# x @ w1 of the second layer of a mixture of experts as Strassen's seven block products over pairs of 512-token tiles

## The chip, the cores and the metric

One core of one Trainium2 chip runs the whole program. The metric is the time of one execution, in microseconds.

## What is computed

A transform of 8 x 3072 tokens of 256 features, then two mixtures of experts over the 24576 tokens, each of 8 experts with w1 of 256 x 1024 and w2 of 1024 x 256. In the first a token goes to one expert; in the second, which the change rewrites, every token goes through all of them and the results are weighted by a matrix P that is balanced in eight iterations.

```python
def _moe2_ref(x, w_gate, w1, w2):
    logits = x @ w_gate
    P = np.exp(logits - logits.max())
    for _ in range(8):
        P /= P.sum(1, keepdims=True) + 1e-09
        P /= P.sum(0, keepdims=True) + 1e-09
        P *= N / E
    for e in range(E):
        h = np.maximum(x @ w1[e], 0.0)
        ye = h @ w2[e]
        out += P[:, e:e + 1] * ye
```

## The kernel before

Products are taken in float32 from two parts: a value is hi + lo, where hi is what TensorE takes in one pass (fp32r), and a product is hi·hi + hi·lo + lo·hi, three matmuls.

The program has three stages, one behind another: the transform with the routing, the first layer (`First`, 50 tiles of 512 tokens that belong to one expert each), and the second layer (`Second`, 48 tiles of 512 tokens by 8 experts). `Second.run` (L792) goes over blocks of `NB` = 3 tiles; for a block it goes over the experts, up in one block and down in the next. Weights of an expert are loaded in two transfers (L707, L709, tiles `r`) and split by POOL (`split`, L490 and L491) for the expert after. For each expert and tile, `hidden` (L508) makes the hidden features, transposed, in 8 chunks of 128: six matmuls of 512 columns into one PSUM bank `ph` (L514), then ACT takes the relu into `hh` (L519) and DVE the rest into `hl` (L520). Then, for each of the tile's four blocks of 128 tokens, 8 chunks by two matmuls: `hh` by w2's hi and lo side by side, 512 columns (L857), and `hl` by w2's hi, 256 columns (L858). DVE adds both halves of the result, weighted by P, to `acc` (L873, L874). Rows of the finished tile are scattered to the output by POOL (L879). A tile's rows are loaded by SP (L803), transposed by PE and split by ACT and DVE (`transposed`, L499 to L503).

P is made in `sinkhorn` (L736): a generator whose steps are mixed into the first two experts of the first block, where results are kept unweighted (L860 to L863). An iteration is eight sums over experts on DVE (L767, L769), a reciprocal, eight products with column sums (L776), and one matmul (L782) that adds the column sums over the partitions.

In the first layer a tile is `hidden` as above and then, for each block of tokens, 8 chunks by three matmuls of 264 columns (L650 to L652). SP's order is the program's there; the other engines' instructions are placed by the scheduler. In the second layer all engines are placed by the scheduler, which keeps no engine's order fixed.

## Time and profile before

| | us |
|---|---|
| median of three runs | 10253.83 |
| lowest, highest | 10252.15, 10259.26 |
| profiled execution (its span) | 10260.5 |

The profile's page starts with the busy time of each engine, then shows the span in 40 slices, the DMA queues, the chain of work that ended last, the costliest groups and the DMA issues. PE is TensorE's matmuls, PEld its loads of stationary operands, DVE VectorE, ACT ScalarE, POOL GpSimd, SP SyncE, and SPq the queue of its DMAs. Groups read `out<-in`, by the names in the program, with partitions x elements. Matmuls overlap: their lengths on the page are longer than the distance between their starts.

### The profile page before, as it was taken

Reading aid. Unit: us, or ns where it says so; the run is one execution under the profiler, and the core shown is the slowest. Engines: PE = TensorE matmul, PEld = TensorE weight load, DVE = VectorE, ACT = ScalarE, POOL = GpSimd, SP = SyncE. Lnnn points to the kernel's source line nnn. Section 1 sums busy time; section 2 is a strip of 40 time slices with the busy share of each in tenths; the row PEclk is TensorE's granted clock in tenths of the full one; section 3 lists DMA queues with packets and bytes.
Section 4 is the critical chain, followed back from the end, with each engine's and each line's share of the span. In section 5 each row is a group of like instructions: output and inputs, shape, how many; then the busy total and the mean of one; then the engine's idle time right before and its main releaser. Section 6 shows DMA issues by size and latency. Waiting matters only on the chain.

```text
span 10260.5 us, 132706 instructions
## 1 busy us (share of the span) xinstructions
PE 10200.5 (99%) x54157; PEld 8686.2 (85%) x54157; DVE 4507.1 (44%) x8480; ACT 2598.8 (25%) x4731; POOL 2714.7 (26%) x2608
## 2 busy tenths in 40 slices
PE   9999999999999999999999999999999999999999
PEld 9799997888888888888888888888888888888888
DVE  5544446444444444444444444444444444444444
ACT  5444442222222222222222222222222222222222
POOL 3655553212222122222122221222212222212221
PEclk9999999999999999999999999999999999999999
DMA  6434442010100010000010000100000101000000
GB/s 174 155 136 138 137 138 78 25 38 33 38 33 30 33 38 33 38 33 36 27 40 31 35 28 33 38 33 38 33 29 33 38 34 38 26 37 33 34 33 15
DMA packets 194250, 525.92 MB, mean 51 GB/s; under 512 B 71617, under 2 KB 128098, under 8 KB 147778
## 3 DMA queue, kind: packets, MB, share of 16 engines
q1 hardware_dynamic: 167440, 464.96, 12.8%
q0 software_dynamic: 25632, 52.25, 1.6%
q8 instruction: 427, 7.00, 0.3%
q14 instruction: 189, 1.55, 0.0%
q10 hardware_dynamic: 562, 0.18, 0.0%
HBM read 433.16 MB, written 84.13 MB: 50 GB/s over the span
## 4 chain that ended last, share of the span: by engine, by line
PE 82%; issue 1%; DVE 0%; POOL 0%; ACT 0%; DMA 0%; POOLq 0%; SPq 0%
PE ph L514 41%; PE py L857 27%; PE py L858 14%; PE pt L501 0%; DVE S L769 0%; DVE P L776 0%; POOL out L879 0%; DVE r L773 0%; POOL w1l L491 0%; DVE acc L862 0%; DMA rows<-x 0%; ACT P L763 0%; DVE hl L520 0%; DVE S L767 0%; POOL w2b L491 0%
## 5 line engine op out<-in xcount | busy, mean ns | idle before, releaser
L519 ACT ACTIVATE hh<-ph 128x512 fp32r<-128x512 f32 x3472 | 2077.0, 598 | 6975.1 <-PE ph L514 6962.5
L520 DVE SCALAR_TENSOR_TENSOR hl<-ph,hh 128x512 fp32r<-128x512 f32 x3472 | 2399.9, 691 | 2922.7 <-ACT hh L519 2916.7
L514 PE MATMUL ph<-xh,w1h 128*128 128x512 f32 x6944 | 2767.4, 399 | 3.0 <-DVE hl L520 2.4
L514 PE MATMUL ph<-xh,w1l 128*128 128x512 f32 x6944 | 2737.2, 394 | 0.0
L514 PE MATMUL ph<-xl,w1h 128*128 128x512 f32 x6944 | 2726.7, 393 | 0.0
L857 PE MATMUL py<-w2a,hh 128*128 128x512 f32 x6144 | 2204.4, 392 | 0.0
L857 PE MATMUL py<-w2b,hh 128*128 128x512 f32 x6144 | 2198.9, 392 | 0.0
L858 PE MATMUL py<-w2a,hl 128*128 128x256 f32 x6144 | 1718.3, 280 | 0.0
L858 PE MATMUL py<-w2b,hl 128*128 128x256 f32 x6144 | 1718.2, 280 | 0.0
L490 POOL CAST w2b<-r 128x512 fp32r<-128x512 f32 x224 | 131.3, 615 | 5771.2 <-PE ph L514 5771.2
L873 DVE SCALAR_TENSOR_TENSOR acc<-py,P,acc 128x256 f32<-128x256 f32 x1332 | 644.0, 483 | 2236.2 <-PE py L858 2236.2
L514 PEld LDWEIGHTS ph<-xh,w1l 128*128 128x128 f32 x6944 | 1304.9, 188 | 332.6
L514 PEld LDWEIGHTS ph<-xh,w1h 128*128 128x128 f32 x6944 | 1304.7, 188 | 303.3 <-DVE hl L520 3.8
L514 PEld LDWEIGHTS ph<-xl,w1h 128*128 128x128 f32 x6944 | 1306.4, 188 | 292.7 <-DVE xl L491 0.5
L857 PEld LDWEIGHTS py<-w2b,hh 128*128 128x128 f32 x6144 | 1153.7, 188 | 254.9
L857 PEld LDWEIGHTS py<-w2a,hh 128*128 128x128 f32 x6144 | 1153.4, 188 | 253.7
L858 PEld LDWEIGHTS py<-w2a,hl 128*128 128x128 f32 x6144 | 1155.4, 188 | 14.2
L858 PEld LDWEIGHTS py<-w2b,hl 128*128 128x128 f32 x6144 | 1153.7, 188 | 0.0
L491 POOL TENSOR_TENSOR w1l<-r,w1h 128x512 fp32r<-128x512 f32 (+1 forms) x550 | 810.3, 1500 | 30.9 <-ACT w1h L490 29.8
L874 DVE SCALAR_TENSOR_TENSOR acc<-py,P,acc 128x256 f32<-128x256 f32 x1512 | 731.6, 484 | 54.0
L650 PE MATMUL py<-w2h,hh 128*128 128x264 f32 x1600 | 458.6, 287 | 0.0
L652 PE MATMUL py<-w2h,hl 128*128 128x264 f32 x1600 | 453.6, 284 | 1.8 <-DVE hl L520 1.8
(179 smaller groups left out, 5756.6 us busy)
## 6 DMA issues: line engine op xcount, KB each, us to landing
r<-m2w SPq DMA_DIRECT2D x226, 1024.0 KB
r<-m1w SPq DMA_DIRECT2D x100, 1024.0 KB
x<-y SPq DMA_DIRECT2D x50, 512.0 KB
xs<-zt SPq DMA_DIRECT2D x64, 384.0 KB
rows<-x SPq DMA_DIRECT2D x48, 512.0 KB
xt<-x SPq DMA_DIRECT2D x31, 768.0 KB
xt<-m1w2t SPq DMA_DIRECT2D x8, 1024.0 KB
tab<-z SPq DMA_DIRECT2D x8, 440.0 KB
```

What stands on the lines that cost most here:

```text
L490: (eng_hi.copy if hasattr(eng_hi, "copy") else eng_hi.tensor_copy)(hi, x)
L491: eng_lo.tensor_tensor(lo, x, hi.bitcast(F32), op=ALU.subtract)
L514: nc.tensor.matmul(p, w[:, k * 1024 + c * 128:k * 1024 + (c + 1) * 128], x[:, k, :], start=(i == 0), stop=(i == 5))
L519: nc.scalar.activation(hh, p, AF.Relu)
L520: nc.vector.scalar_tensor_tensor(hl, p, 0.0, hh.bitcast(F32), op0=ALU.max, op1=ALU.subtract)
L650: nc.tensor.matmul(p, hh, w2h[:, s], start=(c == 0), stop=False)
L652: nc.tensor.matmul(p, hl, w2h[:, s], start=False, stop=(c == 7))
L857: nc.tensor.matmul(p, hh, w2, start=(c == 0), stop=False)
L858: nc.tensor.matmul(p[:, 1, :], hl, w2[:, 0, :], start=False, stop=(c == 7))
L873: nc.vector.scalar_tensor_tensor(dst, p[:, 0, :], pe(e), dst, op0=ALU.mult, op1=ALU.add)
L874: nc.vector.scalar_tensor_tensor(dst, p[:, 1, :], pe(e), dst, op0=ALU.mult, op1=ALU.add)
```

## The change

A group of work is now one pair of tiles (`PAIR` = 8 blocks of 128 tokens), one expert and a quarter of its hidden features (256); 24 x 8 x 4 = 768 groups. Over it, x @ w1 is a product of 2 x 2 blocks: two halves of the 256 input features, two halves of the 256 hidden features, two tiles of tokens. `layer1` makes it from seven products (three matmuls of 512 columns each, L904) instead of eight. Sums of blocks of w1 and of x replace the blocks; sums of products are built in three PSUM banks `a`, `c` and `d`: a bank grows by a second, third or fourth product, and ACT copies it out at two points on the way (`kept`); a second copy goes straight into a sum. DVE adds copies to other banks (`total`, L921, tiles `z`). Of the four blocks of hidden features three come from `z` in SBUF and one from its bank; their relu on ACT and the rest `hl` on DVE (L916) follow.

`layer2` is h @ w2 for a group: for each of 8 blocks of tokens 2 x 3 matmuls of 256 columns (L958) into a half bank of `py`; the banks gather all four groups of an expert, and DVE adds them to `acc` after the fourth (L986). The second half of a group is placed between the products of the next (`turn`). PE's order in the second layer is now the program's (`manual_schedule`).

The seven sums of weight blocks, their hi and lo parts and w2's parts form a piece of 2816 floats on each of 128 partitions for each expert and quarter (`PIECE`). The generator `weights`, mixed into the first layer (`mix`), makes all 32 on ACT and DVE, two at a time, and stores them in DRAM (`wq`). The second layer loads one for each group, again for each pair, into a ring of three tiles. The sums of x are made by `prepare`: four blocks of four transposes, four differences and seven splits, by ACT and DVE for the first and second pair and by POOL for all others. In the first pair the results of experts 0 to 4 are copied to `held` and weighted later (`add_held`); the balancing of P has more, shorter steps, spread over the first groups, and what is left of it is emitted at the start of expert 3 (`HELD - 2`).

```diff
+            late = late(pool("mq", 1))
...
                 next(sp, None)
                 xt = ahead()
+                mix(2)
                 y = yp.tile([128, 4, 264], F32, name="y", tag="y")
...
                     nc.scalar.activation(y[:, j, :], p, AF.Copy, scale=ix[:, j, 2:3].bitcast(F32))
                     next(sp, None)
+                    mix(1)
...
+            def mix(n):
+                for _ in range(n):
+                    next(late, None)
...
-                xt = tile_(i, xt, self.split_weights(i + 1, nc.gpsimd) if i + 1 < NS else late, ahead)
+                xt = tile_(i, xt, self.split_weights(i + 1, nc.gpsimd) if i + 1 < NS else iter(()), ahead)
+            for _ in late:
...
+    def weights(self, pool):
+        store = None
+        for e in range(E):
+            for h in range(2):
...
+                yield
+                yield
+                if store:
+                    store()
+                yield
+                s = pool.tile([128, 2, 4, 128], F32, name="qs", tag="qs")
+                o = pool.tile([128, 2, PIECE], F32R, name="qo", tag="qo")
...
+                tt(s[:, :, 0, :], blk(1, 0), blk(1, 1), op=ALU.add)
+                tt(s[:, :, 1, :], s[:, :, 0, :], blk(0, 0), op=ALU.subtract)
+                yield
+                tt(s[:, :, 2, :], blk(0, 0), blk(1, 0), op=ALU.subtract)
+                tt(s[:, :, 3, :], blk(0, 1), s[:, :, 1, :], op=ALU.subtract)
+                yield
...
+                for hi, lo, v in parts:
+                    nc.scalar.copy(hi, v)
+                    yield
+                    tt(lo, v, hi.bitcast(F32), op=ALU.subtract)
+                    yield
+
+                def store(e=e, h=h, o=o):
+                    nc.sync.dma_start(self.wq[e, 2 * h:2 * h + 2].rearrange("j p c -> p j c"), o.bitcast(F32))
+        store()
...
             for e in range(1, E):
                 nc.vector.scalar_tensor_tensor(S, P[:, e, :], c[:, e:e + 1], S, op0=ALU.mult, op1=ALU.add)
-                if e in (3, 5):
+                if e % 2:
                     yield
             nc.vector.tensor_scalar_add(S, S, 1e-9)
+            yield
             nc.vector.reciprocal(r, S)
             yield
...
                 nc.vector.scalar_tensor_tensor(P[:, e, :], P[:, e, :], c[:, e:e + 1], r, op0=ALU.mult, op1=ALU.mult,
                                                accum_out=cs[:, e:e + 1])
-                if e in (2, 5):
+                if e % 2:
                     yield
+            yield
             yield
             p = psum.tile([128, 512], F32, name="psk", tag="ph")
             nc.tensor.matmul(p[:, 0:E], ones, cs, start=True, stop=True)
...
+            ring, xa, one, rowp, xbp = pool("nw", 3), pool("nxa", 1), pool("n1", 1), pool("nr", 1), pool("nb", 6)
+            ap_, hp, vp, zp = pool("na", 1), pool("nh", 10), pool("nv", 6), pool("nz", 6)
+            ctx.enter_context(tc.manual_schedule(engines={mybir.EngineType.PE}))
+            npair = TPP // PAIR
+            groups = [(b, e, j) for b in range(npair) for e in range(E) for j in range(4)]
+            loads = iter(groups)
+            ready = []
+            def load_weights():
+                g = next(loads, None)
+                if g:
+                    w = ring.tile([128, PIECE], F32R, name="w", tag="w")
+                    nc.sync.dma_start(w.bitcast(F32), self.wq[g[1], g[2]])
+                    ready.append(w)
...
+            def prepare(r, into, fast):
...
+                eh, el = (nc.scalar, nc.vector) if fast else (nc.gpsimd, nc.gpsimd)
+                new = lambda: xbp.tile([128, T], F32, name="xb", tag="xb")
+                def block(k, h):
+                    p = ph.tile([128, T], F32, name="pt", tag="ph")
+                    for i in range(4):
+                        nc.tensor.transpose(p[:, i * 128:(i + 1) * 128], r[:, 4 * h + i, k * 128:(k + 1) * 128], self.cst)
...
+                def keep(m, x):
+                    split(eh, el, hi[:, m, :], lo[:, m, :], x)
...
+                keep(6, b22)
+            def layer1(w, x, h):
+                hi, lo = x
+                wm = lambda part, m: w[:, part * W1P + m * 128:part * W1P + (m + 1) * 128]
+                def product(p, m, first):
+                    for n, (a, v) in enumerate(((0, hi), (0, lo), (1, hi))):
+                        nc.tensor.matmul(p, wm(a, m), v[:, m, :], start=first and n == 0, stop=n == 2,
+                                         skip_group_check=True)
+                def kept(p):
+                    v = vp.tile([128, T], F32, name="v", tag="v")
+                    nc.scalar.copy(v, p)
+                    return v
+                def done(i, half, z):
+                    hh = hp.tile([128, T], F32R, name="hh", tag="hh")
+                    hl = hp.tile([128, T], F32R, name="hl", tag="hl")
+                    nc.scalar.activation(hh, z, AF.Relu)
+                    nc.vector.scalar_tensor_tensor(hl, z, 0.0, hh.bitcast(F32), op0=ALU.max, op1=ALU.subtract)
+                    h[i, half] = hh, hl
+                def total(p, v):
+                    z = zp.tile([128, T], F32, name="z", tag="z")
+                    nc.vector.tensor_tensor(z, p, v, op=ALU.add)
+                    return z
+                new = lambda: ph.tile([128, T], F32, name="ph", tag="ph")
+                a = new()
+                product(a, 0, True)
+                v1 = kept(a)
+                yield
+                c = new()
+                product(c, 1, True)
+                done(0, 0, total(c, v1))
+                yield
+                product(a, 4, False)
+                v2 = kept(a)
+                yield
+                d = new()
+                product(d, 3, True)
+                yield
+                product(a, 5, False)
+                done(1, 1, total(d, kept(a)))
+                yield
+                product(a, 2, False)
+                done(1, 0, a)
+                yield
+                product(d, 6, False)
+                done(0, 1, total(d, v2))
+            def layer2(g, w, h, y, finish):
+                for q in range(PAIR):
+                    s = slice(q % 4 * 128, q % 4 * 128 + 128)
+                    out = y[q // 2][:, q % 2, :]
+                    for i in range(2):
+                        hh, hl = h[i, q // 4]
+                        w2h = w[:, 2 * W1P + i * D:2 * W1P + (i + 1) * D]
+                        w2l = w[:, 2 * W1P + (2 + i) * D:2 * W1P + (3 + i) * D]
+                        for n, (a, v) in enumerate(((hh, w2h), (hh, w2l), (hl, w2h))):
+                            nc.tensor.matmul(out, a[:, s], v, start=g[2] == i == n == q % 2 == 0,
+                                             stop=g[2] == 3 and i == 1 and n == 2, skip_group_check=True)
+                    if g[2] == 3 and q % 2:
+                        finish(q // 2)
+                    yield
...
+            sk = self.sinkhorn(one, hpool, ph, ones)
+            next(sk)
+            for _ in prepare(r, xa, True):
+                pass
+            held = []
+            turn = (0, 2, 0, 1, 2, 1, 2)
...
+            for g in groups:
+                b, e, j = g
+                w, h = ready.pop(0), {}
...
+                if j == 0:
+                    y = [py.tile([128, 2, D], F32, name="py", tag="py") for _ in range(4)]
+                    if b == 0 and e < HELD:
+                        if e == HELD - 2:
+                            for _ in sk:
+                                pass
...
+                    fin = finisher(g, y, acc if b or e >= HELD else None)
+                if (e, j) == (5, 0) and b + 1 < npair:
+                    r = load_rows(b + 1)
+                for n, _ in enumerate(layer1(w, x, h)):
+                    for _ in range(turn[n]):
+                        next(l2, None)
+                    if b == 0:
+                        next(sk, None)
+                        if late and e > HELD and not next(late[0], 1) is None:
+                            late.pop(0)
+                for _ in l2:
                     pass
+                load_weights()
...
+                if b + 1 < npair and (e, j) == ((7, 0) if b == 0 else (6, 0)):
+                    xprep = prepare(r, xb if b % 2 == 0 else xa, b == 0)
+                if e >= 6:
+                    for _ in range(4 if b == 0 else 1):
+                        next(xprep, None)
+                if (e, j) == (E - 1, 3):
+                    for _ in xprep:
                         pass
+                    x = xs.pop(0) if xs else None
+                l2 = layer2(g, w, h, y, fin)
...
+                pass
```

PE's order in a steady group, where `ph_41392` is bank a, `ph_41427` bank d, `w` a piece of weights and `py_40966` two blocks of the group before. Before, a chunk of `hidden` and the start of the next:

```order
L514 MATMUL ph_44716<-xh_42099,w1h_43950 128x512 [waits DVE_49]
L514 MATMUL ph_44716<-xl_42100,w1h_43950 128x512
L514 MATMUL ph_44716<-xh_42099,w1l_43951 128x512
L514 MATMUL ph_44716<-xh_42099,w1h_43950 128x512
L514 MATMUL ph_44716<-xl_42100,w1h_43950 128x512
L514 MATMUL ph_44716<-xh_42099,w1l_43951 128x512
L514 MATMUL ph_44727<-xh_42099,w1h_43950 128x512 [waits DVE_49]
```

Now, from product 4 to product 5:

```order
L904 MATMUL ph_41392<-xh_38062,w_41182 128x512 [waits Activation_49]
L904 MATMUL ph_41392<-xl_38063,w_41182 128x512
L904 MATMUL ph_41392<-xh_38062,w_41182 128x512
L904 MATMUL ph_41427<-xh_38062,w_41182 128x512
L904 MATMUL ph_41427<-xl_38063,w_41182 128x512
L904 MATMUL ph_41427<-xh_38062,w_41182 128x512
L958 MATMUL py_40966<-w_41080,hh_41298 128x256 x2
L958 MATMUL py_40966<-w_41080,hl_41299 128x256
L958 MATMUL py_40966<-w_41080,hh_41355 128x256 x2
L958 MATMUL py_40966<-w_41080,hl_41356 128x256
L904 MATMUL ph_41392<-xh_38062,w_41182 128x512 [waits Activation_49]
```

Six matmuls into one bank and then the next bank became three matmuls into a bank, three into another, one block of tokens of the second half, and the first bank again with a wait for ACT.

DVE's order in the second layer, where `py` are finished rows and `z` the sums that L921 makes. Before, between two tiles:

```order
L871 TENSOR_SCALAR acc_29810<-py_30308,P_21115 128x256 [waits PE_49]
L874 SCALAR_TENSOR_TENSOR acc_29810<-py_30308,P_21115,acc_29810 128x256 [waits DVE_49]
L520 SCALAR_TENSOR_TENSOR hl_30345<-ph_30337,hh_30344 128x512 [waits Activation_49]
L520 SCALAR_TENSOR_TENSOR hl_30356<-ph_30348,hh_30355 128x512 [waits Activation_49]
L520 SCALAR_TENSOR_TENSOR hl_30367<-ph_30359,hh_30366 128x512 [waits Activation_49]
```

Now, in a group that is the first of its expert:

```order
L921 TENSOR_TENSOR z_41334<-ph_41319,v_41332 128x512 [waits Activation_49]
L916 SCALAR_TENSOR_TENSOR hl_41337<-z_41334,hh_41336 128x512 [waits Activation_49]
L916 SCALAR_TENSOR_TENSOR hl_41356<-ph_41286,hh_41355 128x512 [waits Activation_49]
L921 TENSOR_TENSOR z_41368<-ph_41319,v_41317 128x512 [waits PE_49]
L916 SCALAR_TENSOR_TENSOR hl_41371<-z_41368,hh_41370 128x512 [waits Activation_49]
L921 TENSOR_TENSOR z_41402<-ph_41398,v_41396 128x512 [waits PE_49,Activation_49]
L916 SCALAR_TENSOR_TENSOR hl_41405<-z_41402,hh_41404 128x512 [waits Activation_49]
L986 SCALAR_TENSOR_TENSOR acc_38844<-py_40965,P_21425,acc_38844 128x256 [waits PE_49]
```

Where the rests `hl` followed one another, each from its bank, sums `z` stand between them, three of four `hl` read a `z`, and the sums of `acc` come behind, one for a block of tokens instead of two.

DVE's order where the balancing of P runs (`psk` is the bank of column sums, `cc` its reciprocal, `S` the row sums). Before, a whole start of an iteration with other work between:

```order
L783 TENSOR_SCALAR cc_21120<-psk_21575 128x8 [waits PE_49]
L784 RECIPROCAL cc_21120<-cc_21120 128x8 [waits DVE_49]
L785 TENSOR_SCALAR cc_21120<-cc_21120 128x8 [waits DVE_49]
L767 TENSOR_SCALAR S_21117<-P_21115,cc_21120 128x192 [waits DVE_49]
L862 TENSOR_TENSOR acc_21150<-py_21580,acc_21150 128x256 [waits Activation_49]
L769 SCALAR_TENSOR_TENSOR S_21117<-P_21115,cc_21120,S_21117 128x192 [waits DVE_49] x3
L520 SCALAR_TENSOR_TENSOR hl_21611<-ph_21603,hh_21610 128x512 [waits Activation_49]
L769 SCALAR_TENSOR_TENSOR S_21117<-P_21115,cc_21120,S_21117 128x192 [waits DVE_49] x2
L520 SCALAR_TENSOR_TENSOR hl_21622<-ph_21614,hh_21621 128x512 [waits Activation_49]
L769 SCALAR_TENSOR_TENSOR S_21117<-P_21115,cc_21120,S_21117 128x192 [waits DVE_49] x2
```

Now, at expert 3 of the first pair:

```order
L813 TENSOR_SCALAR cc_21430<-psk_22812 128x8 [waits PE_49]
L814 RECIPROCAL cc_21430<-cc_21430 128x8 [waits DVE_49]
L815 TENSOR_SCALAR cc_21430<-cc_21430 128x8 [waits DVE_49]
L795 TENSOR_SCALAR S_21427<-P_21425,cc_21430 128x192 [waits DVE_49]
L797 SCALAR_TENSOR_TENSOR S_21427<-P_21425,cc_21430,S_21427 128x192 [waits DVE_49] x7
L800 TENSOR_SCALAR S_21427<-S_21427 128x192 [waits DVE_49]
L802 RECIPROCAL r_21428<-S_21427 128x192 [waits DVE_49]
L805 SCALAR_TENSOR_TENSOR P_21425,cs_21431<-P_21425,cc_21430,r_21428 128x192 [waits DVE_49]
L805 SCALAR_TENSOR_TENSOR P_21425,cs_21431<-P_21425,cc_21430,r_21428 128x192 x7
L813 TENSOR_SCALAR cc_21430<-psk_22835 128x8 [waits PE_49]
```

The sums `hl` and of `acc` that stood between the steps are gone from there; an iteration stands whole, and the next behind it.

PE's order at the same places. Before, with one matmul of column sums:

```order
L857 MATMUL py_21580<-w2b_19587,hh_21456 128x512
L782 MATMUL psk_21575<-cs_21121,ones_81 128x8 [waits DVE_49]
L858 MATMUL py_21580<-w2b_19587,hl_21457 128x256
L857 MATMUL py_21580<-w2b_19587,hh_21467 128x512
L858 MATMUL py_21580<-w2b_19587,hl_21468 128x256
L514 MATMUL ph_21603<-xh_21471,w1h_19584 128x512 [waits Activation_49]
```

Now:

```order
L958 MATMUL py_22355<-w_22350,hl_22645 128x256
L812 MATMUL psk_22812<-cs_21431,ones_73 128x8
L812 MATMUL psk_22835<-cs_21431,ones_73 128x8 [waits DVE_49]
L812 MATMUL psk_22858<-cs_21431,ones_73 128x8 [waits DVE_49]
L812 MATMUL psk_22881<-cs_21431,ones_73 128x8 [waits DVE_49]
L904 MATMUL ph_22895<-xh_21436,w_22584 128x512 [waits DMAHW3_49]
```

One matmul among those of the second half became four in a row, three of them waiting for DVE, ahead of the next group's first product.

## Rows read from the trace of the kernel before

**Rows 1.** Page: busy time, chain that ended last, a group, DMA issues

```profile
PE 10200.5 (99%) x54157; PEld 8686.2 (85%) x54157; DVE 4507.1 (44%) x8480; ACT 2598.8 (25%) x4731; POOL 2714.7 (26%) x2608
...
PE 82%; issue 1%; DVE 0%; POOL 0%; ACT 0%; DMA 0%; POOLq 0%; SPq 0%
...
L874 DVE SCALAR_TENSOR_TENSOR acc<-py,P,acc 128x256 f32<-128x256 f32 x1512 | 731.6, 484 | 54.0
...
r<-m2w SPq DMA_DIRECT2D x226, 1024.0 KB
```

**Rows 2.** Timeline of PE, second layer: start, length (us), engine, line, operation

```profile
5002.11 0.39 PE L857 MATMUL py<-w2a,hh 128*128 128x512 f32 x1
...
5013.20 0.39 PE L514 MATMUL ph<-xh,w1h 128*128 128x512 f32 x1
...
5024.39 0.39 PE L857 MATMUL py<-w2a,hh 128*128 128x512 f32 x1
```

**Rows 3.** Timeline of PE, first layer: 24 matmuls of 264 columns between

```profile
1000.48 0.28 PE L650 MATMUL py<-w2h,hh 128*128 128x264 f32 x1
...
1003.38 0.39 PE L514 MATMUL ph<-xh,w1h 128*128 128x512 f32 x1
```

**Rows 4.** Timeline of all engines, first layer; in brackets idle time before, releaser

```profile
1004.54 0.40 PE L514 MATMUL ph<-xh,w1l 128*128 128x512 f32 x1
...
1004.98 0.60 ACT L519 ACTIVATE hh<-ph 128x512 fp32r<-128x512 f32 x1 [0.91 <-PE ph L514]
...
1005.61 0.69 DVE L520 SCALAR_TENSOR_TENSOR hl<-ph,hh 128x512 fp32r<-128x512 f32 x1 [10.42 <-ACT hh L519]
```

**Rows 5.** One line's instructions: shortest/median/longest ns, first and last start, shapes

```profile
L769 DVE SCALAR_TENSOR_TENSOR S<-P,cc,S x56: 401/419/1341, 1655.4 to 1777.0; 128x192 f32<-128x192 f32 x56
...
L491 POOL TENSOR_TENSOR w1l<-r,w1h x550: 1279/1302/2435, 437.2 to 10116.6; 128x512 fp32r<-128x512 f32 x151, 128x1024 fp32r<-128x1024 f32 x33
L491 DVE TENSOR_TENSOR xl<-pt,xh x196: 672/678/692, 432.4 to 9707.0; 128x512 fp32r<-128x512 f32 x196
L491 DVE TENSOR_TENSOR w2l<-g,w2h x50: 217/2452/2453, 363.7 to 1575.0; 128x64 fp32r<-128x64 f32 x50
```

**Rows 6.** One tile's instructions: issues of the raw weights, 3000 to 3600

```profile
L707 SPq DMA_DIRECT2D r<-m2w x7: 327/328/328, 3063.6 to 3534.3; - x7
L709 SPq DMA_DIRECT2D r<-m2w x7: 382/384/425, 3064.1 to 3534.7; - x7
```

**Rows 7.** Stretches: PE, PEld, DVE, ACT, POOL busy; granted clock, DMA share, GB/s

```profile
3066.00:3067.00 1.00, 1.00 (x6) 0.81 (x5) 0.69 (x1) 0.22 (x1) 1.00 (x2) 1.00 0.97 410
3070.00:3071.00 1.00, 1.00 (x6) 0.79 (x5) 0.69 (x1) 0.20 (x2) 0.00 (x0) 1.00 0.18 74
```

**Rows 8.** Timeline of DVE, first layer, one tile behind the last of rows 4

```profile
1029.28 0.69 DVE L520 SCALAR_TENSOR_TENSOR hl<-ph,hh 128x512 fp32r<-128x512 f32 x1 [10.42 <-ACT hh L519]
```

**Rows 9.** Timeline where the second layer starts (1615 to 1645)

```profile
1622.58 0.28 PE L652 MATMUL py<-w2h,hl 128*128 128x264 f32 x1
...
1629.62 0.82 SPq L803 DMA_DIRECT2D rows<-x  x2
...
1633.31 1.94 PE L501 MATMUL pt<-ident,rows 128*128 128x128 f32 x8 [10.45 <-DMA rows<-x]
```

**Rows 10.** Waits of PE: waiting group, releaser: us in all, count, longest

```profile
PE psk L782 <- DVE P L776: 8.1, 2, 6.3
```

**Rows 11.** Timeline of DVE, balancing of P (1655 to 1690)

```profile
1674.68 0.15 DVE L783 TENSOR_SCALAR cc<-psk 128x8 f32<-128x8 f32 x1
...
1676.47 0.42 DVE L862 TENSOR_TENSOR acc<-py,acc 128x256 f32<-128x256 f32 x1
...
1684.25 0.17 DVE L783 TENSOR_SCALAR cc<-psk 128x8 f32<-128x8 f32 x1
```

**Rows 12.** Stretches, columns as in rows 7: the start of the second layer

```profile
1626.00:1628.00 2.00, 0.00 (x0) 0.00 (x0) 0.00 (x0) 0.00 (x0) 0.00 (x0) 0.56 0.30 52
1636.00:1638.00 2.00, 2.00 (x9) 1.65 (x9) 0.96 (x2) 0.28 (x1) 0.00 (x0) 0.88 1.04 410
```

More of the change, by code (lines that the diff above doesn't have):

```diff
@@ new lines, in run, with load_rows @@
+            npair = TPP // PAIR
[8 more added lines that the diff above has]
+                    ready.append(w)
+            def load_rows(b):
+                r = rowp.tile([128, PAIR, D], F32, name="rows", tag="rows")
+                for h in range(2):
+                    nc.sync.dma_start(r[:, 4 * h:4 * h + 4, :], x1v[:, PAIR * b + 4 * h:PAIR * b + 4 * h + 4, :])
+                return r
@@ L893, in body @@
+            for _ in l2:
+                pass
 def body(tc, x, embT, tau, m1w1, m1w2, m1w2t, wg, m2w1, m2w2, c_f96, c_fcs, c_cs, c_m12, c_tok, c_kc, c_nt, out):
     nc = tc.nc
-    with tc.tile_pool(name="dram", bufs=1, space=DRAM) as dp, tc.tile_pool(name="keep", bufs=1) as keep, \
-            tc.tile_pool(name="small", bufs=3) as small, tc.tile_pool(name="mi", bufs=4) as ixp, \
-            tc.tile_pool(name="big", bufs=10) as big:
+    from contextlib import ExitStack
+    with tc.tile_pool(name="dram", bufs=1, space=DRAM) as dp, tc.tile_pool(name="keep", bufs=1) as keep:
```

246 lines of the change are left out of this document (118 added, 128 removed).

## The prediction

> **What bounds the kernel now.** The page was read first, then starts of single instructions in both layers, then the places where PE waits. PE is busy 99% of the span, and the chain of work that ended last is 82% PE [rows 1]; the rest is the transform ahead and short waits. So in the second layer time is matmul pace. A matmul's length on the page overlaps the next one's; the pace is start to start. One tile of 512 tokens through one expert runs from 5002.11 to 5024.39, 22.28 us, in two halves: 32 pairs of a 512-column and a 256-column matmul in 11.09 us (0.3466 a pair), then 48 matmuls of 512 columns in 11.19 us (0.2331 each) [rows 2]. 48 tiles by 8 experts make 384 x 22.28 = 8556 us, and PE's busiest part has no gap for another engine to fill: only fewer columns help.
>
> **What the change does to PE.** A group is now one pair of tiles, one expert, 256 hidden features. Its x @ w1 was 2 chunks x 2 tiles x 6 = 24 matmuls of 512 columns and is 7 products x 3 = 21. Its second half was 16 pairs of 512 + 256 columns and is 48 matmuls of 256: the same 12,288 columns in narrower pieces. 21 x 0.2331 = 4.895 us. A run of 256-column matmuls isn't in the trace before. The nearest row is the first layer: 24 matmuls of 264 columns in the same order (hh, hh, hl) in 2.90 us, 0.1208 each [rows 3]; by columns that is 0.1208 x 256/264 = 0.1172, which I take, since it is nearest in shape and order. Lower end: 0.3466 - 0.2331 = 0.1135 (what a 256-column matmul adds to a pair). Upper end: 0.1208, if narrow matmuls have a floor and don't get cheaper by columns. A group is 4.895 + 48 x 0.1172 = 10.52 us (10.34 to 10.69); 24 pairs x 8 experts x 4 = 768 groups make 8080 us (7943 to 8212). **Against 8556 that is -476 us** (-613 to -344). Transposes stay at 384 blocks of 128 columns, also on PE.
>
> **Waits that the change adds in a group.** PE now keeps the order of the program, so what waits holds all matmuls behind it. Bank a takes products 0, 4, 5 and 2 in turn, and ACT must copy it out before it grows. In the new order of PE in a steady group, between product 4 and product 5 stand product 3 (0.70 us) and one block of tokens of the second half (6 x 0.1172 = 0.70): 1.40 us. The copy needs, by the first layer's relu, 0.21 us from the time that the last matmul gives way (it started at 1004.54, 0.23 earlier than that; ACT started at 1004.98) and 0.60 us of ACT [rows 4]; with 0.1 us back to PE (my estimate: DVE follows ACT 0.03 us after its end there) 0.9 us. Spare: 0.5 us. Between products 5 and 2 stand two blocks, 1.41 us: the same spare. Bank d's second product waits for copy and DVE's sum, 0.9 + 0.68 [rows 5] + 0.05 = 1.6 us, under 2.8 us of other matmuls. ACT has 7 x 0.60 = 4.2 us of work in 10.5, DVE 4 x 0.69 + 3 x 0.68 = 4.8 us, and in each expert's first group 8 x 0.48 us of sums of y (L874) [rows 1] more, 8.7 us. All fit, so I take 0 for the waits, with the relay of the copies as a rival below.
>
> **Weights from DRAM.** SP issues 768 loads of 1.44 MB. A load waits for the last matmul that reads the piece three groups earlier and must land before the group after next starts: one group, 10.5 us. Behind it on SP stand only later loads and, once a pair, two of rows that are due 40 us later. Two loads of 1024 KB [rows 1] were issued at 3063.6 and 3064.1 [rows 6]; the 16 engines moved 410 GB/s at 3066 and were nearly done by 3070 to 3071 [rows 7]: 2.1 MB in 6.6 us with its latency. 1.44 MB at 410 GB/s is 3.5 us, 4.7 to 6.6 us in all. PE hides it; cost 0.
>
> **Single costs.** (1) First layer: 16 pieces of weights, each four ACT casts (2816 columns, some 3.3 us) and eight DVE operations (3840 columns, some 5 us at 0.68 a 512), over 30-odd tiles. DVE idles 10.42 us of each 23.67 us tile [rows 8]: +3 us (0 to 50). (2) Start: before, PE stood from 1622.9 to 1633.31 for the rows [rows 9]. Now 1.05 MB of rows and 1.44 MB of weights come first, 2.5/0.41 + 2 = 8 us from the issue at 1629.62, so the first product is due at 1638 where the first hidden matmul came behind the transposes, at 1633.31 + 1.94 = 1635.25; making seven sums of x takes ACT 11 x 0.6 = 6.6 us against 4.9 us of products; the logits land behind all three weight pieces, and PE's order has their transpose at the end of group 0. Together +10 us (5 to 20). (3) The balancing of P: PE waited 8.1 us for it before [rows 10]. Its four iterations among the first groups add 3.5 us of DVE to 4.8 in each 10.5 us: +2 us net (-8 to +15). But at expert 3 all that is left is emitted at once: the new order at expert 3 shows three whole iterations on DVE and three matmuls of PE that wait for them, one behind another, ahead of the next product. One iteration ran from 1674.68 to 1684.25, 9.57 us with three sums of y of 0.42 us in it (one stands in the rows), so 8.3 us [rows 11]: PE stands 3 x 8.3 = 25 us. PE's clock fell to half after the stand at 1623 and came back 3 us after its restart [rows 9, 12]: +1.5. So +27 us with rounding up (20 to 37). (4) The second pair's x is made by ACT and DVE in two groups, beside the last sums of the held y: 6.6 us on each: +7 us (0 to 15). Later pairs' x is made by POOL over eight groups, 11 x 1.3 + 7 x 0.6 = 18.5 us in 84: 0.
>
> **Sum.** -476 + 3 + 10 + 2 + 27 + 7 = -427 us: the profiled execution, whose own time is its span of 10260.5, would take 9834 us. The median of the runs, 10253.8, is 6.7 us under that span, so I predict **9827 us**.
>
> **Rivals.** *Narrow matmuls have a floor.* For it: 0.1208 is all that the trace shows of a run of them, and every matmul loads its own stationary. Against: in the pairs a 256-column matmul adds only 0.1135. It gives 48 x 0.0036 x 768 = +133: 9960 us.
>
> *POOL holds DVE.* Three of four hl come from z, so both inputs lie in SBUF (L916 with hl<-z in the new order of DVE); before, one was PSUM. A DVE sum of 64 columns with both inputs in SBUF took 2452 ns beside a POOL sum of as much, and the balancing sums went from 419 to 1341 ns, while PSUM sums never left 672 to 692 [rows 5]. POOL runs 11 sums of 1.3 us for each of 23 pairs. If each held PE for its length, 11 x 1.3 x 23 = +329: 10156 us; the spare of 1.2 us on bank d and PE's blocks in between should take most of it, and a half would give 9990. The Trainium skill, SBUF — State Buffer, section Who interferes with whom, says that a VectorE operation with two SBUF inputs and a GpSimd operation that reads SBUF exclude each other, the later one waiting for the whole of the earlier; by that rule all 11 do block DVE, and the trace agrees (2452 ns).
>
> *No gain: the copies' relay is late.* If a copy took 1.7 us from bank to bank where 0.9 is worked out, PE would wait 0.3 us twice a group, 0.6 x 768 = +430: the time of before. Against: hundreds of reliefs of the same length in the first layer, with PE never waiting.
>
> *Slower: the ring of three.* With L from release to landing and 10.52 us of matmuls, a group takes (10.52 + L)/2 once L exceeds 10.52, as each load has one group to come in. The gain left after the single costs is 427/768 = 0.556 us a group, so from L = 11.63 us the kernel is slower; at 13 us it takes 9827 + 1.24 x 768 = 10779 us. It would need under a third of the rate in [rows 7]; writes of rows and scattered output come once a pair only.
>
> **Chances.** Forecast 0.80 (9720 to 9930), floor 0.08, POOL 0.06 (9900 to 10156), no gain 0.02, slower 0.04. A range of 9720 to 9965 holds the first two and some of the third. Faster by over 0.2% 0.94, within 0.2% (about what a measurement of this kernel tells from no change) 0.02, slower 0.04.
>
> **What would show it.** Starts of narrow matmuls 0.117 us apart inside a block and products 0.233 apart; groups of 10.5 us from first product to first product; PE's waits for ACT copies and for the weight loads near zero outside the first pair; three PE waits of 8 to 9 us on the P update some 130 us into the second layer, with the clock at half behind; the DMA rate near 137 GB/s (1.44 MB in 10.52 us) on average with gaps between loads. I am wrong if the weight load ends PE's idle time, if groups at experts 6 and 7 of later pairs are longer than others by more than the transposes, or if the first layer's tile grows over 23.67 us.

## The result, and the profile after

The changed kernel takes 9832.17 us (median of four runs, 9825.52 to 9833.35) where the kernel before takes 10256.55 beside it (10252.15 to 10260.76): a ratio of 0.9583, 95% interval 0.9569 to 0.9596, that is 4.2% less; the two medians lie 424 us apart. The forecast was 9827. The profiled execution of after has a span of 9830.5 us, 430.0 under that of before.

From the page of after: busy time, the chain that ended last, the DMA issue of the weight pieces.

```profile
PE 9738.7 (99%) x64141; PEld 8860.9 (90%) x64141; DVE 5265.9 (54%) x9298; ACT 4081.6 (42%) x7105; POOL 1504.8 (15%) x1204
...
PE 79%; issue 4%; DVE 0%; DMA 0%; POOL 0%; ACT 0%; SPq 0%; POOLq 0%; DVEq 0%; ACTq 0%
...
w<-wqd SPq DMA_DIRECT2D x768, 1408.0 KB
```

Beside [rows 1]: PE is 99% busy as before, in a span that is 430 us shorter; ACT's busy time grew by 1480 us and DVE's by 760, and none of it shows in the chain. What bounds the kernel is still the pace of matmuls.

The first product of a group and of the next, in an even pair (the first two rows) and in an odd one (the last two); between the first two, two starts of a block of tokens' six narrow matmuls. Timeline of PE, after:

```profile
3794.97 0.40 PE L904 MATMUL ph<-xh,w 128*128 128x512 f32 x1
...
3796.34 0.40 PE L958 MATMUL py<-w,hh 128*128 128x256 f32 x2
...
3797.04 0.40 PE L958 MATMUL py<-w,hh 128*128 128x256 f32 x2
...
3805.44 0.40 PE L904 MATMUL ph<-xh,w 128*128 128x512 f32 x1
...
4133.09 0.40 PE L904 MATMUL ph<-xh,w 128*128 128x512 f32 x1
...
4143.69 0.40 PE L904 MATMUL ph<-xh,w 128*128 128x512 f32 x1
```

Six narrow matmuls take 0.70 us, 0.117 each. A group takes 10.47 us in the even pair and 10.60 in the odd one; this holds for every steady group (one beside which no x is made and P isn't balanced) of all 24 pairs (10.474 and 10.600), and the forecast's 10.52 lies between. In even pairs a wide matmul takes 230.3 ns from start to start and a narrow one 117.4; in odd ones 233.3 and 118.8. That every second pair is slower was in no row of before, where all tiles behind the first seven and away from changes of block took 22.29 us. It became a question of the experiments.

Where the layers meet and where the program ends (timelines of PE, after; then the same two places before):

```profile
1619.23 0.28 PE L654 MATMUL py<-w2h,hl 128*128 128x264 f32 x1
1630.52 3.55 PE L861 MATMUL pt<-ident,rows 128*128 128x128 f32 x16 [11.01 <-DMA rows<-x]
1636.19 0.47 PE L904 MATMUL ph<-xh,w 128*128 128x512 f32 x1 [2.12 <-ACT xh L490]
...
9817.65 0.28 PE L958 MATMUL py<-w,hl 128*128 128x256 f32 x1
```

```profile
1635.12 1.22 PE L514 MATMUL ph<-xh,w1h 128*128 128x512 f32 x2
...
10251.74 0.28 PE L858 MATMUL py<-w2b,hl 128*128 128x256 f32 x1
```

With [rows 9] these give the account of the 430 us. Times are of the profiled executions:

| stretch | before | after | difference |
|---|---|---|---|
| start to the first layer's last matmul | 1622.6 | 1619.2 | -3.4 |
| from there to the first matmul of x @ w1 | 12.5 | 17.0 | +4.4 |
| steady matmuls: 384 x 22.286; 384 x 10.474 + 384 x 10.600 | 8557.9 | 8092.4 | -465.5 |
| over that up to the last matmul | 58.7 | 89.1 | +30.4 |
| last matmul to the end | 8.7 | 12.9 | +4.2 |

### The profile page after: what moved, and what is told of

Read it like the earlier page. It is cut to its first block, busy times and chain, and to the rows that moved or that the text cites. A ratio compares the mean times of both kernels' runs of the same rounds, so it can differ in the third digit from the quotient of the medians.

```text
span 9830.5 us, 155094 instructions
## 1 busy us (share of the span) xinstructions
PE 9738.7 (99%) x64141; PEld 8860.9 (90%) x64141; DVE 5265.9 (54%) x9298; ACT 4081.6 (42%) x7105; POOL 1504.8 (15%) x1204
## 4 chain that ended last, share of the span: by engine, by line
PE 79%; issue 4%; DVE 0%; DMA 0%; POOL 0%; ACT 0%; SPq 0%; POOLq 0%; DVEq 0%; ACTq 0%
PE py L958 42%; PE ph L904 36%; PE pt L861 0%; DMA lraw<-lgd 0%; DVE S L797 0%; POOL out L990 0%; DVE P L805 0%; DVE r L802 0%; ACT P L791 0%; ACT hh L915 0%; POOL xl L491 0%; DVE z L921 0%; PE psk L812 0%; DVE mx L776 0%; POOL xb L868 0%
## 5 line engine op out<-in xcount | busy, mean ns | idle before, releaser
L958 PE MATMUL py<-w,hh 128*128 128x256 f32 x24576 | 4524.3, 281 | 0.0
L958 PEld LDWEIGHTS py<-w,hh 128*128 128x128 f32 x24576 | 4027.7, 188 | 334.3
L904 PE MATMUL ph<-xh,w 128*128 128x512 f32 x10752 | 4002.4, 395 | 3.8 <-ACT xh L490 2.1
L958 PE MATMUL py<-w,hl 128*128 128x256 f32 x12288 | 3446.6, 280 | 0.0
L921 DVE TENSOR_TENSOR z<-ph,v 128x512 f32<-128x512 f32 x2304 | 1590.7, 690 | 2333.0 <-ACT v L909 1836.0
L916 DVE SCALAR_TENSOR_TENSOR hl<-z,hh 128x512 fp32r<-128x512 f32 x2304 | 1645.4, 714 | 1364.6 <-ACT hh L915 1364.3
L958 PEld LDWEIGHTS py<-w,hl 128*128 128x128 f32 x12288 | 2322.9, 189 | 0.0
L904 PEld LDWEIGHTS ph<-xh,w 128*128 128x128 f32 x10752 | 2022.1, 188 | 311.0 <-ACT xh L490 2.4
L904 PE MATMUL ph<-xl,w 128*128 128x512 f32 x5376 | 2116.3, 394 | 0.2 <-DVE xl L491 0.2
L904 PEld LDWEIGHTS ph<-xl,w 128*128 128x128 f32 x5376 | 1015.8, 189 | 69.1 <-DVE xl L491 0.7
L986 DVE SCALAR_TENSOR_TENSOR acc<-py,P,acc 128x256 f32<-128x256 f32 x1304 | 566.8, 476 | 21.7 <-PE py L958 2.4
L520 DVE SCALAR_TENSOR_TENSOR hl<-ph,hh 128x512 fp32r<-128x512 f32 x400 | 272.9, 688 | 532.1 <-ACT hh L519 526.3
L916 DVE SCALAR_TENSOR_TENSOR hl<-ph,hh 128x512 fp32r<-128x512 f32 x768 | 530.7, 691 | 38.8 <-ACT hh L915 0.3
```

The lines of the kernel that those rows point to most:

```text
L520: nc.vector.scalar_tensor_tensor(hl, p, 0.0, hh.bitcast(F32), op0=ALU.max, op1=ALU.subtract)
L904: nc.tensor.matmul(p, wm(a, m), v[:, m, :], start=first and n == 0, stop=n == 2, skip_group_check=True)
L916: nc.vector.scalar_tensor_tensor(hl, z, 0.0, hh.bitcast(F32), op0=ALU.max, op1=ALU.subtract)
L921: nc.vector.tensor_tensor(z, p, v, op=ALU.add)
L958: nc.tensor.matmul(out, a[:, s], v, start=g[2] == i == n == q % 2 == 0, stop=g[2] == 3 and i == 1 and n == 2, skip_group_check=True)
L986: nc.vector.scalar_tensor_tensor(acc[:, q, :], y[i][:, q % 2, :], pe(e, q), acc[:, q, :], op0=ALU.mult, op1=ALU.add)
```

## The experiments

A time with a range is the median of four or five runs, one without is a single run. Runs of one kernel lie up to 12 us apart here, so what matters below that is read from starts in the traces.

**An eighth product.** The first product is made twice.

```diff
                 product(a, 0, True)
+                product(a, 0, True)
                 v1 = kept(a)
```

> Product 0 is made twice in each group, so 24 matmuls of 512 columns where the changed kernel has 21; nothing else differs. Theory (PE's pace is the whole of it, and the gain is the three matmuls saved): +3 x 0.232 us x 768 groups = +534 us on 9832, so about 10366, slower than the kernel before, with a group of 11.17 us in even and 11.30 in odd pairs. Rival (PE hides work behind waits for copies or for the weight loads): the extra product falls into slack and costs under half of that, below 10100.

It took 10363.2 us, +531. Two successive groups start here (timeline of PE, an even pair):

```profile
3900.64 0.40 PE L904 MATMUL ph<-xh,w 128*128 128x512 f32 x1
...
3911.79 0.40 PE L904 MATMUL ph<-xh,w 128*128 128x512 f32 x1
```

11.15 us, 0.68 more than 10.47. There is no slack on PE, and the saved eighth is the whole of the gain: with eight products the new structure (narrow second half, streamed weights, a program's order) is slower than the kernel before.

**Less cover for a copy.** The block of tokens between products 3 and 5 goes behind product 5.

```diff
-            turn = (0, 2, 0, 1, 2, 1, 2)
+            turn = (0, 2, 0, 0, 3, 1, 2)
```

> The one block of tokens between products 3 and 5 is moved behind product 5, so only product 3 (0.70 us) covers ACT's copy of bank a. Theory (relay of 0.9 us from the last matmul's giving way to the next product): PE waits 0.2 us in each of 768 groups, +154 us, 9986. Rival 1 (the relay takes 1.4 us, the spare was used up): +0.7 x 768 = +540 us, 10370. Rival 2 (a relay under 0.70): no change, 9832.

It took 10062.5 us, +230. Two successive groups start here (timeline of PE, an even pair):

```profile
3853.57 0.40 PE L904 MATMUL ph<-xh,w 128*128 128x512 f32 x1
...
3864.35 0.40 PE L904 MATMUL ph<-xh,w 128*128 128x512 f32 x1
```

A group takes 10.78 us: 0.31 us of wait. The waits of PE's weight loads show who is late (waiting group, releaser: us in all, count, longest):

```profile
PEld ph L904 <- ACT v L909: 365.4, 768, 1.9
```

The loads stand 0.48 us a group, of which 0.31 reaches the matmuls. After has 2.0 us and 2 waits in that row. So the relay from product 4 through ACT's copy to product 5 takes 0.70 + 0.31 = 1.0 us where 0.9 was worked out, and the order as changed has 0.4 us to spare, not 0.5.

**The balancing of P, spread out.** In after, PE stands three times at expert 3 (timeline of PE, then stretches with the granted clock in the third column from the end):

```profile
1779.97 0.59 PE L812 MATMUL psk<-cs,ones 128*128 128x8 f32 x2 [9.27 <-DVE P L805]
1789.32 0.59 PE L812 MATMUL psk<-cs,ones 128*128 128x8 f32 x2 [8.75 <-DVE P L805]
1798.66 0.59 PE L812 MATMUL psk<-cs,ones 128*128 128x8 f32 x2 [8.75 <-DVE P L805]
```

```profile
1800.00:1808.00 8.00, 8.00 (x39) 7.12 (x39) 3.25 (x10) 2.95 (x5) 0.00 (x0) 0.72 0.00 0
...
1803.00:1804.00 1.00, 1.00 (x7) 1.00 (x7) 0.49 (x1) 0.48 (x1) 0.00 (x0) 0.50 0.00 0
...
1805.00:1806.00 1.00, 1.00 (x7) 0.83 (x6) 0.00 (x0) 0.79 (x2) 0.00 (x0) 1.00 0.00 0
```

```diff
-                        if e == HELD - 2:
-                            for _ in sk:
-                                pass
```

> The lines that emit all that is left of the balancing of P at expert 3 are taken out; its steps go on, one behind each product, and end in the first group or two of expert 4, before P is first used. Theory (PE stands 3 x 8.9 us there and restarts at half clock): the group of 39.2 us and the one of 13.0 behind it become 10.5 to 10.7, -31 us, 9801. Rival (the steps between the products hold z and hl on DVE, so the stand is only spread out): at most -10 us, 9822 or more.

It took 9801.8 us (9801.5 to 9804.4), 0.9555 of before (0.9540 to 0.9571): -30. The same two groups start here now, and the one behind them:

```profile
1762.38 0.40 PE L904 MATMUL ph<-xh,w 128*128 128x512 f32 x1
...
1772.85 0.40 PE L904 MATMUL ph<-xh,w 128*128 128x512 f32 x1
...
1783.58 0.40 PE L904 MATMUL ph<-xh,w 128*128 128x512 f32 x1
```

The groups of 39.17 and 13.04 us are now 10.47 and 10.73. The steps had room between the products all along. Emitting them at once cost 31 us: 26.8 of standing, 1.9 in which the matmuls of column sums themselves ran (some 0.6 each), and 2.3 of half clock, which lasted for 5.4 us behind the restart at 1799.1.

**The place of x.** Four runs add unused tiles of some bytes between the others, to find out why odd pairs are slower. x of the even pairs and of the odd pairs lies in two different places; everything else a group uses is the same. The first moved both places (and all behind the first by 64):

```diff
+            pool("npa", 1).tile([128, 8], F32, name="pa", tag="pa")
             xa = pool("nxa", 1)
+            pool("npb", 1).tile([128, 8], F32, name="pb", tag="pb")
...
+                    pool("npc", 1).tile([128, 8], F32, name="pc", tag="pc")
                     xb = pool("nxb", 1)
```

> Two unused tiles of 32 bytes shift x of the even pairs from address 51360 to 51392 and x of the odd pairs from 182784 to 182880 in each partition (all that lies behind moves by 64). In the changed kernel a steady group takes 10.474 us in even and 10.600 in odd pairs. Theory A (the place of x against a boundary of 64 bytes sets the pace): the two change places, 10.600 even and 10.474 odd, time about the same. Theory B (the far region of the memory is slower, or the pace has nothing to do with x's address): 10.474 and 10.600 stay.

> Only unused bytes between the tiles. A piece of weights lies at 17568, 28832 or 40096 in each partition: remainder 32 by 128. x of the even pairs, fast in the changed kernel at 51360 (remainder 32), goes to 51488 (still 32 by 128, but 288 instead of 160 by 1024); x of the odd pairs, slow at 182784 (remainder 0), goes to 184480 (32 by 128 and 160 by 1024). Theory C (x with the remainder of the weights by 128 is fast): 10.47 in both, about 9784. Theory C' (the remainder by 1024 counts): even 10.6, odd 10.47, about 9832. Theory D (a near region is fast, a far one slow, whatever the remainder): odd stays 10.6.

> Unused bytes put the pieces of weights, x of both kinds of pairs and the hidden features at multiples of 128. Theory C (equal remainders of weights and x are fast, whatever they are): 10.47 in both kinds of pairs, about 9784. Rival (a remainder of 32 itself is fast, 0 is slow): 10.6 in both, about 9880.

> Unused bytes move the hidden features hh and hl, and what lies behind them, by 64, while the weights and x of both kinds of pairs keep the remainders by 1024 at which a group took 10.474 us (160 for all three). Theory E (a matmul's pace goes by its own operands' places): the 48 matmuls that read hh and hl go from 117.4 to over 118.5 ns and the 21 of the products stay at 230.3; group 10.53, about 9826. Rival (the hidden features' place is of no matter, only x's against the weights'): 10.474 in both kinds of pairs, 9784.

They took 9885.0, 9805.7, 9884.6 and 9890.2 us. The other three differ in the bytes and places of the unused tiles alone: the second has 128, 896 and 672 bytes at the three places of the first, the third 96 ahead of the weights and 32 behind x of the even pairs, the fourth 64 behind x of the even pairs and 608 ahead of x of the odd ones. Starts of successive groups: in the second, an odd pair; in the third, an even one; in the fourth, an even one.

```profile
4127.70 0.40 PE L909 MATMUL ph<-xh,w 128*128 128x512 f32 x1
...
4138.17 0.40 PE L909 MATMUL ph<-xh,w 128*128 128x512 f32 x1
```

```profile
3811.30 0.40 PE L909 MATMUL ph<-xh,w 128*128 128x512 f32 x1
...
3821.94 0.40 PE L909 MATMUL ph<-xh,w 128*128 128x512 f32 x1
```

```profile
3812.62 0.40 PE L908 MATMUL ph<-xh,w 128*128 128x512 f32 x1
...
3823.24 0.40 PE L908 MATMUL ph<-xh,w 128*128 128x512 f32 x1
```

All kinds of pairs together, with the remainders by 1024 of the addresses of a weight piece, x and the hidden features, and the means over 12 steady groups:

| kernel, pairs | weights | x | hidden | wide, ns | narrow, ns | group, us |
|---|---|---|---|---|---|---|
| after, even | 160 | 160 | 512 | 230.3 | 117.4 | 10.474 |
| after, odd | 160 | 512 | 512 | 233.3 | 118.8 | 10.600 |
| first, even | 160 | 192 | 576 | 232.2 | 119.7 | 10.620 |
| first, odd | 160 | 608 | 576 | 233.1 | 118.7 | 10.593 |
| second, even | 160 | 288 | 512 | 231.9 | 117.8 | 10.527 |
| second, odd | 160 | 160 | 512 | 230.3 | 117.4 | 10.474 |
| third, even | 256 | 256 | 640 | 231.6 | 120.2 | 10.633 |
| third, odd | 256 | 640 | 640 | 231.2 | 119.3 | 10.580 |
| fourth, both | 160 | 160 | 576 | 233.1 | 119.1 | 10.613 |

The first run gave neither theory A nor B: even pairs went to 10.620 us, and odd ones to 10.593, far from the 10.474 of theory A. The second settles the question that it was made for: with x of the odd pairs at the remainder of the even ones, and still in the far region, the group is 10.474 to the digit. So it is the place, not the region (theory D fell) and not the work of odd pairs. Nor is it the chip: the four runs, the spread balancing and the last experiment were made on three, and 10.474 came out on all three. No rule for it came out. Equal remainders of weights and x aren't enough (second and third, even: theories C and C' fell). A remainder of 32 by 128 isn't what is fast, though the third run's time is what that rival gave (9880): in the second run's even pairs and in the fourth x has it too, at 10.527 and 10.613. And a matmul's own operands don't decide (fourth: theory E fell and its rival with it, since the products got slower though their weights and x kept their remainders; what moved by 64 were the tiles behind x of the even pairs, the hidden features among them. In odd pairs of after the narrow matmuls are slower though only x lies elsewhere). What decides stays open.

**A warmer start.**

```diff
+            p = ph.tile([128, T], F32, name="pw", tag="ph")
+            for _ in range(80):
+                nc.tensor.matmul(p[:, :128], self.cst, self.cst, start=True, stop=True)
...
-                    if b == 0:
+                    if b == 0 and (e, j) != (0, 0):
                         next(sk, None)
```

> On top of the spread balancing (9801.8): 80 matmuls of 128 columns on PE while the first rows come, and the balancing's first step comes a group later. Theory (PE waits 5.5 us for the maximum of the logits and runs at half clock behind its stand): that wait goes, the 16 transposes take 1.9 instead of 3.6 us, the first group 8 to 10 instead of 16.4 and the second 10.5 instead of 12.6 us: -10 to -14, about 9790. Rival (the first products wait for ACT's and DVE's making of x, 6.6 us): no more than the 5.5 us of the wait go, 9796.

It took 9808.3 us (9801.0 to 9812.0), no better than 9801.8 without. The wait for the logits is gone (5.5 us), the 16 transposes take 1.91 us instead of 3.65, and the second group takes 10.57 us instead of 12.61, but the first group takes 16.0 us where it took 16.4, and the third 11.7 instead of 10.5. The stands for x bring the half clock back that the warm start had taken away. Waits of PE, then stretches:

```profile
PE ph L904 <- DVE xl L491: 3.8, 1, 3.8
PE ph L904 <- ACT xh L490: 2.9, 2, 2.4
```

```profile
1638.00:1640.00 2.00, 0.00 (x0) 0.00 (x0) 2.00 (x2) 0.00 (x0) 0.00 (x0) 1.00 0.93 364
...
1646.00:1648.00 2.00, 2.00 (x6) 1.54 (x5) 1.15 (x2) 0.86 (x2) 0.00 (x0) 0.50 0.00 0
```

The rival was right in kind: the first products wait for x, and earlier waits only hid it. In the profile of this run first product to fourth group is 38.3 us instead of 39.5; a gain of that size is under what these runs can tell.

**Twice the work on POOL.**

```diff
-                    el.tensor_tensor(t, x, y, op=ALU.subtract)
+                    for _ in range(1 if fast else 2):
+                        el.tensor_tensor(t, x, y, op=ALU.subtract)
...
-                    split(eh, el, hi[:, m, :], lo[:, m, :], x)
+                    for _ in range(1 if fast else 2):
+                        split(eh, el, hi[:, m, :], lo[:, m, :], x)
```

> POOL makes every difference, copy and rest of x twice in 22 of the pairs: 37 us of POOL work in their 84 us instead of 18.5. Theory (POOL does hold DVE, but what DVE has spare takes it): groups of experts 6 and 7 get at most 0.2 us longer, 0 to +15 us in all, 9832 to 9847. Rival (PE waits whenever POOL holds DVE): 11 more holds of 1.3 us in 22 pairs, +315 us, or a half of that, 9990 to 10147.

It took 9833.7 us, +1.5, which a single run can't tell from nothing; but in the traces pairs 3 to 24 take 7446.4 us in both kernels, from first product to the start of the last group, the same to the ns. POOL does hold DVE all the same. In after (timeline of POOL and DVE):

```profile
5003.71 1.30 POOL L868 TENSOR_TENSOR xb<-xb 128x512 f32<-128x512 f32 x1 [8.83 <-ACT xb L863]
5004.52 0.69 DVE L921 TENSOR_TENSOR z<-ph,v 128x512 f32<-128x512 f32 x1 [1.19 <-PE ph L904]
...
5005.76 1.29 POOL L491 TENSOR_TENSOR xl<-xb,xh 128x512 fp32r<-128x512 f32 x1
5005.90 1.70 DVE L916 SCALAR_TENSOR_TENSOR hl<-z,hh 128x512 fp32r<-128x512 f32 x1 [0.70 <-ACT hh L915]
```

`hl<-z`, with both inputs in SBUF, took 1.70 us where its median is 0.69; `z<-ph,v`, with one in PSUM, took its 0.69 beside a POOL sum. The Trainium skill, SBUF — State Buffer, section Who interferes with whom, says that a VectorE instruction with two SBUF inputs contends with a GpSimd instruction that reads SBUF, and the trace agrees. 87 of the 3072 `hl` in after took over 0.75 us, 52 us over in all, and 197 here, 113 us over; PE lost nothing by either.

**The second half in wide pieces.**

```diff
-                        for n, (a, v) in enumerate(((hh, w2h), (hh, w2l), (hl, w2h))):
-                            nc.tensor.matmul(out, a[:, s], v, start=g[2] == i == n == q % 2 == 0,
-                                             stop=g[2] == 3 and i == 1 and n == 2, skip_group_check=True)
+                        w2 = w[:, 2 * W1P:].rearrange("p (h i d) -> p h i d", h=2, i=2)[:, :, i, :]
+                        nc.tensor.matmul(y[q // 2], hh[:, s], w2, start=g[2] == i == q % 2 == 0, stop=False,
+                                         skip_group_check=True)
+                        nc.tensor.matmul(out, hl[:, s], w2[:, 0, :], start=False,
+                                         stop=g[2] == 3 and i == 1, skip_group_check=True)
```

> The second half as before the change: 16 pairs of a 512-column matmul (both parts of w2) and one of 256 instead of 48 of 256. Both parts go to one bank, so two blocks of tokens are added up there and the output isn't the layer's; columns and everything off PE are the same. Theory (the narrow pieces cost a little by their number): 16 x 0.3466 = 5.55 us where the 48 take 5.64 (even) and 5.70 (odd), -0.12 us x 768 = -95 us, 9737. Rival (pace goes by columns alone): 9832.

It took 9767.5 us, -65, between the two. Two successive groups of an even pair start here:

```profile
3780.43 0.40 PE L904 MATMUL ph<-xh,w 128*128 128x512 f32 x1
...
3790.86 0.40 PE L904 MATMUL ph<-xh,w 128*128 128x512 f32 x1
```

A group takes 10.434 us in even and 10.473 in odd pairs, 0.083 less in the mean; 16 wide pairs take 5.55 to 5.58 us, 48 narrow ones 5.64 to 5.70. So columns in narrow pieces cost some 2% more here, at 117.4 to 118.8 ns and not the 120.8 of the floor among the prediction's rivals. The place of tiles alone does as much to narrow matmuls (117.4 to 120.2), so one placement doesn't settle how much of the 2% is owed to their width. Half of the gain was lost in even pairs: the products, which the edit doesn't touch, went from 230.3 to 232.4 ns there (in odd pairs 233.3 to 233.1). So the pace of a matmul isn't a matter of place alone: the matmuls around it count too.

**A ring of two pieces.**

```diff
-            ring, xa, one, rowp, xbp = pool("nw", 3), pool("nxa", 1), pool("n1", 1), pool("nr", 1), pool("nb", 6)
+            ring, xa, one, rowp, xbp = pool("nw", 2), pool("nxa", 1), pool("n1", 1), pool("nr", 1), pool("nb", 6)
...
-            for _ in range(3):
+            for _ in range(2):
                 load_weights()
```

> The ring holds two pieces instead of three, so a load starts when the last matmul of the group two earlier is done and has no other group to hide behind. Theory (a load takes 5 us from issue to landing, as the trace's transfer from 5002.6 to 5007.5): a group takes 10.5 + 5, 15.5 us, 768 x 5 = +3840 us, 13700. Rival (the load is slower than its busy time shows, hidden by the third tile): 10.5 + 8 or more, above 16000. If the load were no matter at all: 9832.

It took 16161.8 us, 18.9 a group. The wait for weights and the clock (waits of PE; stretches, columns as in [rows 7]):

```profile
PE ph L904 <- DMA w<-wqd: 4608.9, 765, 8.1
```

```profile
6006.00:6008.00 2.00, 0.00 (x0) 0.00 (x0) 0.00 (x0) 0.00 (x0) 0.00 (x0) 1.00 0.94 400
6008.00:6010.00 2.00, 0.14 (x1) 0.15 (x1) 0.00 (x0) 0.00 (x0) 0.00 (x0) 0.62 0.52 220
6010.00:6012.00 2.00, 2.00 (x5) 1.61 (x6) 0.00 (x0) 0.41 (x1) 0.00 (x0) 0.50 0.00 0
...
6016.00:6018.00 2.00, 2.00 (x13) 1.76 (x12) 0.00 (x0) 0.59 (x1) 0.00 (x0) 1.00 0.00 0
```

The wait is 4608.9 / 765 = 6.0 us a group, near the 5 expected. The other 2.3 us are the clock: behind a stand of 6 us PE runs for 3 to 6 us at 0.5 (1.2 GHz), 4.4 in the mean, and the mean clock over the run is 0.833. The theory had left that out, and its 13700 missed by 2460. The time is what the rival gave, but not for its reason: the slow load isn't there, 400 GB/s move while it runs. The third tile hides all of it in after, where a load is issued at 5002.60 and its traffic ends before 5008, some 5 us ahead of its need:

```profile
5007.00:5008.00 1.00, 1.00 (x8) 0.93 (x8) 0.60 (x1) 0.21 (x1) 0.05 (x1) 1.00 0.48 203
5008.00:5009.00 1.00, 1.00 (x8) 0.89 (x7) 0.00 (x0) 0.32 (x1) 0.00 (x0) 1.00 0.00 0
```

**Both gains together.** The balancing spread, and x of the odd pairs at 184480.

> The balancing spread as in the third run, and x of the odd pairs placed at 184480 as in the fifth, where a steady group took 10.474 us. Theory (the two gains are independent and add up): 12 odd pairs x 32 groups x 0.126 = -48 us on 9801.8, 9753. Rival (the place works only beside the other addresses of the fifth run): 10.5 to 10.6 in odd pairs, 9780 to 9802.

It took 9756.6 us (9747.8 to 9759.9), 0.9504 of before (0.9491 to 0.9517): 76 us under the changed kernel. Starts of successive groups, an odd pair:

```profile
4094.26 0.40 PE L908 MATMUL ph<-xh,w 128*128 128x512 f32 x1
...
4104.73 0.40 PE L908 MATMUL ph<-xh,w 128*128 128x512 f32 x1
```

The steady group is 10.474 us in all pairs; the two gains add up.

## Why the prediction was right

- **The pace and the matmul term.** -476 us was forecast, -465.5 measured. The price of a wide matmul (0.2331) was 3 ns too high in even pairs and right in odd ones; a narrow one was taken at 117.2 ns and took 117.4 and 118.8. The eighth product shows that the gain is matmuls saved: put back, they cost 531 us where the change gained 424. The forecast knew nothing of the two paces; their mean happens to lie 0.017 us over its 10.52.
- **Waits inside a group: 0.** Right, with a spare of 0.4 us for bank a's copy instead of 0.5.
- **Weights: 0.** Right: PE never waits for a piece. The 5 us lie within the 4.7 to 6.6 worked out from [rows 7]; exposed, the load costs 6.0, and the clock 2.3 more.
- **First layer: +3.** Four of its tiles take 24.17 us instead of 23.67, +2.0, one of the forecast's own signs of being wrong, though a small one. The stage as a whole still ended 3.4 us earlier, which the forecast hadn't: it begins 0.9 us earlier, its first tile takes 25.6 us where it took 26.5, and the last 22.7 where it took 26.3 before, when the splitting of the second layer's first weights was mixed into it. That this is the reason is argued and not shown.
- **Start, balancing's early part and second pair: +10, +2, +7; the stand at expert 3: +27.** Together +46 forecast. Measured: the stretch to the first product +4.4, and the first pair 48.4 us over its steady groups (its first group has no second half, which is added here) against 19.4 for the first seven tiles before: +33.4. The stand's share was too small, 31 instead of 27: an iteration took 8.9 us and not 8.3 (26.8 for the 25), the matmuls of column sums themselves 1.9, which the sum left out, and the half clock 2.3 for the 1.5. The second pair's x cost 2.9 us, transposes included, and not 7. And the forecast didn't set against its terms all that before had lost there: its 8.1 us of waits [rows 10] are less than half of the 19.4.
- **Not in the forecast:** the end, +4.2. The last eight blocks of rows leave POOL one behind another, 1.28 us apart, in a pair's last group.

The single errors, +10.5 on matmuls, -12.6 on the first pair, -6.4 on the first layer, +4.2 at the end and +1.4 on transposes, add up to -3. The total is nearer than the steps deserve: steps of some 10 us are what this reading can do.

Of the rivals, *POOL holds DVE* has its mechanism as described and no price (no ns in 22 pairs for twice the work). *Narrow matmuls have a floor* was given 133 us over the sum's 117.2 ns and came to 0.9 ns in the mean of both paces, 34 us; the 65 us of the wide pieces are counted from wide ones, and most of them lie in the 117.2 ns already. *The relay* is 1.0 us and *the ring* 5 to 6, both short of the points from which they decide. The relay's price has a slip: 0.6 x 768 is 461 and not 430, which is slower than before and not the same time. The forecast doesn't rest on it.

## What to carry to other kernels

Where PE is busy 99% of the time, price a change in matmuls by starts to starts of the nearest shape, and spend the rest of the care on what the new program order makes PE wait for: a helper's leftover work that is emitted at once (here three iterations on DVE, 31 us) costs its whole length and half clock behind it, and goes away when it is dealt out one step a product. Leave a streamed load one whole stage of cover; an uncovered load costs its time and the clock besides. And when equal work runs at two paces in two places of memory, move the tiles by some bytes and measure again.

## What the runs showed of the hardware that was not expected

The pace of the same matmuls in the same order differs by up to 1.5% (10.474 to 10.633 us a group) with the place of tiles in SBUF, down to shifts of 64 bytes, wide and narrow matmuls alike, at a granted clock of 1.00 throughout. It is the same to a few ns in every group of a placement, and each of a group's 69 matmuls starts at the same distance from the one ahead to about 1 ns in every group: a fixed rhythm and not chance delays. Each group of the table is a whole number of steps of 1/150 us (the fast one, 10.4733 us, is 1571 steps, 10.600 is 1590, 10.580 is 1587); why isn't known. It doesn't come from what POOL does: with twice its work the groups kept their times. Worth 45 us here, it was found only because two places alternate; a kernel with one place would never have shown it.
